# Recomputing two operand sums on VectorE instead of parking them in DRAM, and respacing the inner products of a Strassen-style token MLP

## The chip, the cores and the metric

The kernel runs on one core of a Trainium2 chip. The time is device microseconds (us) of that core, as the median of several executions. The profile's span, from the first to the last instruction, is about 2 us shorter than this time. A program on one core has no second, slower state to be told apart by its dies; every run used here was classed as fast, with a granted TensorE clock of 0.996 to 1.0. The executions at 0.996 or 0.997 are among the longest of their kernel (e11, which is after once more: 576.9 us at 0.997, 574.84 to 575.15 at 1.0). In the profile of that one the MLP starts 2.0 us later than in after, at 237.37 against 235.35 us, and its stages agree with those of after within 0.01 us. So medians and upper ends carry this difference at the start; the lengths of stages do not.

## The reference

The block is a linear attention layer, then a token-mixing MLP, each with a residual. Shapes: S = 2048 tokens, D = 1024, F = 3584, bfloat16. Only the second half matters here:

```
h  = x + attention(layernorm(x))
n  = layernorm(layernorm(h))              # S x D
u  = gelu(einsum("sd,sf->df", n, w1) + b1)   # first MLP matmul
y  = einsum("df,fs->ds", u, w2) + b2         # second MLP matmul
out = h + transpose(y)
```

## The kernel before

Both MLP matmuls are done by Strassen-Winograd products: seven products (1 to 7) of 128-row blocks instead of eight. The moving operand of the second matmul is g, the GELU output, kept as even rows `gE` and odd rows `gO`. Products 6, 7 and 4 need sums T2, T3 and T4 of g's blocks. `combine` makes them, row pair by row pair, as the first matmul ends each one:

```python
def combine(e, o, t2, t3, t4):
    lo, hi = slice(0, CW), slice(CW, 2 * CW)
    sub = ALU.subtract
    nc.vector.tensor_tensor(t3, o[:, hi], e[:, hi], sub)
    nc.vector.tensor_tensor(e[:, hi], e[:, hi], e[:, lo], sub)
    nc.vector.tensor_tensor(t2, o[:, hi], e[:, hi], sub)
    if t4 is not None:
        nc.vector.tensor_tensor(t4, o[:, lo], t2, sub)
# ... class Mixer1 (first matmul): after product 4 of row pair p
def done(self):
    p = self.p
    if p < NFP - 2:
        sg = stg.tile([P, 3, CW], FP16, tag="sg", name="sg")
        combine(gE[:, p, :], gO[:, p, :], sg[:, 0, :], sg[:, 1, :], sg[:, 2, :])
        nc.sync.dma_start(g_park[0][:, p, :, :], sg[:])      # parked in DRAM
```

The three sums are not kept in SBUF side by side: T2 is loaded once, and T3 and T4 take turns in one pair of tiles, reloaded from DRAM each time:

```python
def stream(m, t):                    # m = 7: T3, m = 4: T4
    def load():
        ts = stream_tiles()          # one buffer of each half
        nc.sync.dma_start(ts[0][:], g_park[0][:, 0:H2, t, :])
        # ... two more loads for the other half
        bind(m, ts)
    return load
```

Row pairs are worked in quads (two pairs). In a quad, products 1 and 5 of the two pairs together (in the second matmul only product 5) are themselves replaced by seven half-size inner products i1 to i7 (256 columns). These share two PSUM banks and hand partial sums on by ScalarE copies, so plain matmuls (512 columns) are placed between them:

```python
lo, hi = list(range(nk // 2)), list(range(nk // 2, nk))
def halves(fs):
    hs = [lambda f=f, ks=ks: f(ks) for f in fs for ks in (lo, hi)]
    return hs + [nop] * (4 - len(hs))
def interleave(n, fs):               # fs: products of the two pairs
    x = halves(fs)
    for f in (n.i1, x[0], n.i6, n.i2, x[1], n.i5, n.i7, x[2], n.i3, x[3], n.i4):
        f()
```

In the first matmul each x is 4 plain matmuls. The order of instructions on each engine is set by a scheduler that follows the program's order only loosely. The second matmul opens with two pairs done one after the other (`run_pair`), then runs quads.

## Time and profile before

Median 582.98 us (582.48 to 584.5, 4 runs). Three lines of the page: the span, the busy time of each engine, and the busy share of the DMA engines in 40 slices of the span, in tenths.

```profile
span 580.8 us, 8190 instructions
...
PE 568.5 (98%) x3061; PEld 287.2 (49%) x3061; DVE 363.0 (63%) x755; ACT 252.5 (43%) x547; POOL 1.8 (0%) x8
...
DMA  9934321149428652105144160549798897886415
```

Matmuls look 98% busy, but that hides gaps. One 128x512 matmul is recorded at 379 ns while matmuls in a run start 216 ns apart, so an idle stretch of up to 0.16 us disappears under the tail of the matmul before. The Trainium skill ("Perfetto Trace Analysis", "Identifying the Most-Contended Engine") says as much: matmul busy share is not a good measure of the distance to the limit. I therefore compare the time of a stage with its matmul count at the observed rates (about 216 ns for 512 columns and 109 ns for 256; the last column uses unrounded rates).

| stage of before | start, us | takes, us | at the observed rates, us |
|---|---|---|---|
| opening pairs of the first matmul | 235.54 | 23.97 | 22.44 |
| quad 1 (one pending pair) | 259.51 | 23.01 | 21.6 |
| quad 2 | 282.52 | 23.52 | 23.34 |
| quads 3, 4, 5 | 306.04 | 24.27, 24.40, 24.40 | 23.34 each |
| quad 6 and the last product 4 | 379.11 | 27.66 | 26.8 |
| first pairs of the second matmul, up to its first inner product | 406.77 | 51.97 | 48.35 |
| two steady quads of the second matmul | 458.74 | 41.61, 41.60 | 41.6 |

The windows view of before; columns are the stretch, its length, busy us of each engine with counts, clock, DMA share, GB/s. The rows are quads 3 to 5, the first pairs of the second matmul, and its two steady quads.

```profile
core 0: us, PE busy (x) PEld busy (x) DVE busy (x) ACT busy (x) POOL busy (x), PEclk, DMA share, GB/s
...
306.04:379.11 73.07, 71.70 (x410) 39.88 (x409) 43.87 (x97) 32.84 (x73) 0.00 (x0) 1.00 0.36 119
406.77:458.74 51.97, 49.25 (x226) 21.90 (x225) 30.96 (x41) 5.28 (x9) 0.00 (x0) 1.00 0.92 261
458.74:541.95 83.21, 83.21 (x435) 42.46 (x434) 39.72 (x52) 8.22 (x18) 0.00 (x0) 1.00 0.81 232
```

The largest MLP waits of the matmul engine (who waited, for what: total us, times, longest):

```profile
PE psC_4755 L285 <- DMA gs_4704<-g_park_2908: 0.8, 1, 0.8
...
PE psA_2922 L285 <- ACT psB_2923 L304: 0.7, 1, 0.7
PE psC_4610 L285 <- ACT psC_4610 L321: 0.7, 1, 0.7
...
PE psC_4755 L285 <- DMA gs_4798<-g_park_2908: 0.5, 1, 0.5
...
PE psI_3799 L218 <- ACT psA_3795 L419: 0.3, 1, 0.3
```

`gs` are the reloaded sums. The timeline of the start of quad 4, with the matmul engine's idle time in brackets:

```profile
330.31 0.60 PE L218 MATMUL psI_3799<-hE,wq 128*128 128x256 f16 x4
330.75 1.03 PE L285 MATMUL psC_3668<-hT_2232,wq 128*128 128x512 f16 x4
331.99 0.60 PE L218 MATMUL psI_3800<-hi_2916,is 128*128 128x256 f16 x4 [0.21 <-ACT psI_3800 L228]
...
332.86 1.03 PE L285 MATMUL psC_3668<-hT_2232,wq 128*128 128x512 f16 x4
334.17 0.60 PE L218 MATMUL psI_3799<-hE,is 128*128 128x256 f16 x4 [0.28 <-ACT psA_3795 L419]
```

i6 should have followed the four plain matmuls at 331.61 and started at 331.99. i5 should have started at 333.72 and started at 334.17. Both wait for ScalarE copies (L228, L419).

### The profile page before, as it was taken

Reading aid. Unit: us, or ns where it says so; the run is one execution under the profiler, and the core shown is the slowest. Engines: PE = TensorE matmul, PEld = TensorE weight load, DVE = VectorE, ACT = ScalarE, POOL = GpSimd, SP = SyncE. Lnnn points to the kernel's source line nnn. Section 1 sums busy time; section 2 is a strip of 40 time slices with the busy share of each in tenths; the row PEclk is TensorE's granted clock in tenths of the full one; section 3 lists DMA queues with packets and bytes.
Section 4 is the critical chain, followed back from the end, with each engine's and each line's share of the span. In section 5 each row is a group of like instructions: output and inputs, shape, how many; then the busy total and the mean of one; then the engine's idle time right before and its main releaser. Section 6 shows DMA issues by size and latency. Waiting matters only on the chain.

```text
span 580.8 us, 8190 instructions
## 1 busy us (share of the span) xinstructions
PE 568.5 (98%) x3061; PEld 287.2 (49%) x3061; DVE 363.0 (63%) x755; ACT 252.5 (43%) x547; POOL 1.8 (0%) x8
## 2 busy tenths in 40 slices
PE   8999999999999999999999999999998999999997
PEld 3444444455554444345555455554443554544544
DVE  6898878556678889774755738452575328236323
ACT  5657777756668767444535354354110110100100
POOL 1000000000000000000000000000000000000000
PEclk9999999999999999999999999999999999999999
DMA  9934321149428652105144160549798897886415
GB/s 305 351 69 90 93 55 37 20 150 311 82 57 166 173 170 85 43 29 172 32 168 143 57 200 28 172 126 314 196 300 278 271 305 235 228 229 217 146 31 169
DMA packets 119784, 91.52 MB, mean 158 GB/s; under 512 B 32818, under 2 KB 112192, under 8 KB 119744
## 3 DMA queue, kind: packets, MB, share of 16 engines
q1 hardware_dynamic: 119008, 90.32, 54.2%
q10 hardware_dynamic: 672, 0.66, 0.3%
q8 instruction: 24, 0.39, 0.3%
q14 instruction: 16, 0.13, 0.1%
q0 software_dynamic: 64, 0.01, 0.0%
HBM read 70.00 MB, written 13.63 MB: 144 GB/s over the span
## 4 chain that ended last, share of the span: by engine, by line
PE 73%; DMA 10%; DVE 9%; ACT 4%; issue 2%; SPq 0%; ACTq 0%; DVEq 0%
PE acc_t L963 9%; PE acc_t L1111 9%; DMA wq<-in_B_w_dram 6%; PE psB L694 4%; PE psC L694 4%; PE psA L694 4%; DVE sa L277 2%; PE psE L694 2%; PE nd_ps L1062 1%; DMA xr<-in_A_x_dram 1%; PE psC_4610 L285 1%; DMA gs_4633<-g_park_2908 1%; ACT gO L355 1%; PE psB_4544 L285 1%; PE psA_5495 L285 1%
## 5 line engine op out<-in xcount | busy, mean ns | idle before, releaser
L285 PEld LDWEIGHTS <-sa 128*128 128x128 f16 x716 | 70.0, 98 | 80.1 <-issue 3.8
L285 PEld LDWEIGHTS <-wq 128*128 128x128 bf16 x590 | 57.2, 98 | 63.0 <-issue 2.5
L963 PE MATMUL acc_t<-xnT,wq_sb 128*128 128x512 bf16 x256 | 58.0, 379 | 0.0
L1111 PE MATMUL acc_t<-wo_sb,pqT 128*128 128x512 bf16 x256 | 56.1, 379 | 0.0
L277 DVE TENSOR_TENSOR sa<-wq 128x1024 f16<-128x1024 bf16 (+1 forms) x44 | 36.1, 829 | 19.6 <-DMA wq<-in_B_w_dram 14.9
L1111 PEld LDWEIGHTS <-pqT 128*128 128x128 bf16 x256 | 24.9, 98 | 29.0
L963 PEld LDWEIGHTS <-wq_sb 128*128 128x128 bf16 x256 | 24.5, 98 | 27.4
L166 ACT ACTIVATE e_sb<-acc_t 128x512 bf16<-128x512 f32 x40 | 23.9, 597 | 26.6 <-PE acc_t L963 24.3
L218 PEld LDWEIGHTS <-is 128*128 128x128 f16 x276 | 26.9, 97 | 16.9 <-issue 6.3
L170 DVE TENSOR_SCALAR e_sb<-e_sb 128x512 bf16<-128x512 bf16 x64 | 18.5, 289 | 25.3 <-ACT e_sb L166 24.8
L694 PEld LDWEIGHTS <-xs 128*128 128x128 f16 x208 | 20.1, 98 | 23.3 <-DVE xs L680 1.3
L694 PE MATMUL psA<-wkv,xnT 128*128 128x512 bf16 x104 | 26.7, 379 | 0.0
L1122 DVE BATCH_NORM_STATS2 hst<-acc_t 128x6 f32<-128x512 f32 x32 | 22.1, 693 | 6.7 <-ACT h_bf L1121 6.5
L1109 ACT CAST acc_t<-xr 128x512 f32<-128x512 bf16 x32 | 19.0, 593 | 13.4 <-DVE hst L1122 13.3
L277 DVE TENSOR_TENSOR sa<-wq,sa 128x1024 f16<-128x1024 bf16 (+1 forms) x22 | 18.3, 830 | 10.4 <-PE psI_4907 L218 3.1
L694 PEld LDWEIGHTS <-xnT 128*128 128x128 bf16 x156 | 15.3, 98 | 18.5 <-issue 0.2
L167 ACT ACTIVATE r_sb<-acc_t 128x512 bf16<-128x512 f32 x40 | 23.7, 593 | 0.0
L618 PE MATMUL acc_t<-wkv,xnT 128*128 128x512 bf16 x96 | 21.6, 379 | 0.7 <-ACT xnT L871 0.7
L1083 DVE TENSOR_TENSOR o_sb<-nd_ps,rd 128x384 bf16<-128x384 f32 (+1 forms) x48 | 21.7, 504 | 0.6 <-ACT rd L1078 0.4
L587 DVE BATCH_NORM_STATS2 st<-x_sb 128x6 f32<-128x512 bf16 x32 | 20.5, 681 | 1.6 <-DMA x_sb<-in_A_x_dram 1.6
L1121 ACT CAST h_bf<-acc_t 128x512 bf16<-128x512 f32 x32 | 18.4, 574 | 1.0 <-PE acc_t L1111 0.9
L277 DVE TENSOR_TENSOR sa<-sa,wq 128x1024 f16<-128x1024 f16 (+1 forms) x22 | 18.2, 829 | 0.0
(711 smaller groups left out, 959.0 us busy)
## 6 DMA issues: line engine op xcount, KB each, us to landing
wq<-in_B_w_dram SPq DMA_DIRECT2D x14, 1024.0 KB, 7.9
wq<-in_B_w_dram SPq DMA_DIRECT2D x8, 1792.0 KB, 12.1
g_park_2908<-sg SPq DMA_DIRECT2D x12, 384.0 KB, 3.8
xr<-in_A_x_dram SPq DMA_DIRECT2D x16, 256.0 KB, 3.0
out_dram<-ot SPq DMA_DIRECT2D x31, 128.0 KB, 3.4
x_sb<-in_A_x_dram SPq DMA_DIRECT2D x15, 256.0 KB, 3.3
wkv<-in_A_wqkv_dram SPq DMA_DIRECT2D x2, 1024.0 KB, 9.0
wq_sb<-in_A_wqkv_dram SPq DMA_DIRECT2D x2, 1024.0 KB, 13.6
```

The source lines that it names most:

```text
L166: pin(nc.scalar.activation(e_sb[:], src, ACT.Exp))
L167: pin(nc.scalar.activation(r_sb[:], src, ACT.Relu))
L218: nc.tensor.matmul(ps, lhsT=self.lhs[m][:, k, :], rhs=self.mov[m][:, k, :], start=(start and k == 0), stop=(k == self.nk - 1), skip_group_ ...
L277: return nc.vector.tensor_tensor(t, a, b, op)
L285: nc.tensor.matmul(ps[:, cols], lhsT=lhs[:, k, :], rhs=mv(k)[:, cols], start=(start and k == 0), stop=(k == self.nk - 1), skip_group_check ...
L587: return nc.vector.bn_stats(st[:, c, :], x_sb[:, c * CW:(c + 1) * CW])
L618: mm = nc.tensor.matmul(pp[:, 0:CW], lhsT=xnT[:, kt, i * P:(i + 1) * P], rhs=wkv[:, kt, c * CW:(c + 1) * CW], start=(kt == 0), stop=(kt == ...
L694: pin(nc.tensor.matmul(ps[:], lhsT=lhs[:, k, :], rhs=rhs[:, k, :], start=(start and k == 0), stop=(k == hk2 - 1), skip_group_check=True,))
L963: nc.tensor.matmul(qp[:, 0:SW], lhsT=wq_sb[:, kt, j * P:(j + 1) * P], rhs=xnT[:, kt, u * SW:(u + 1) * SW], start=(kt == 0), stop=(kt == ND ...
L1083: nc.vector.tensor_tensor(o_sb[:, b * JPB * P:(b * JPB + nsl) * P].rearrange("p (s h e) -> p s h e", h=HB, e=DH), blk[:, :, 0:P].rearrange ...
L1111: nc.tensor.matmul(ap_[:, 0:CW], lhsT=pqT[:, j, i * P:(i + 1) * P], rhs=wo_sb[:, j, dc * CW:(dc + 1) * CW], start=(j == 0 and not SEED_RES ...
L1122: nc.vector.bn_stats(st[:, dc, :], ap_[:, 0:CW])
```

## The change

The intent is to stop parking T2, T3 and T4. Only the in-place subtraction stays in the first matmul. T2 is made once on VectorE at the switch. T3 and T4 are made anew for each quad, in place of each reload. The plain matmuls between the inner products are spread 5, 4, 3, 4. Two smaller reorderings come along: the first two pairs of the second matmul go jointly, and in opening pairs product 2 is split around product 6. Cut to its core:

```diff
         def done(self):
-            p = self.p
-            if p < NFP - 2:
-                sg = stg.tile([P, 3, CW], FP16, tag="sg", name="sg")
-                combine(gE[:, p, :], gO[:, p, :], sg[:, 0, :], sg[:, 1, :], sg[:, 2, :])
-                nc.sync.dma_start(g_park[0][:, p, :, :], sg[:])
+            e = gE[:, self.p, :]
+            nc.vector.tensor_tensor(e[:, CW:D], e[:, CW:D], e[:, 0:CW], ALU.subtract)
 ...
             def interleave(n, fs):
-                x = halves(fs)
-                for f in (n.i1, x[0], n.i6, n.i2, x[1], n.i5, n.i7, x[2], n.i3, x[3], n.i4):
-                    f()
+                steps = [(f, k) for f in fs for k in range(nk)]
+                t = len(steps)
+                cuts = [0, (5 * t + 8) // 16, (9 * t + 8) // 16, (12 * t + 8) // 16, t]
+                ...                      # fill(q) runs steps[cuts[q]:cuts[q + 1]]
+                for f in (n.i1, 0, n.i6, n.i2, 1, n.i5, n.i7, 2, n.i3, 3, n.i4):
+                    fill(f) if isinstance(f, int) else f()
 ...    # run_pair without a pending pair
-            for ks in (head, last):
-                st.p5(ks)
-                st.p2(ks)
+            st.p5(list(range(st.nk - 1)))
+            st.p2(list(range(h)))
+            st.p5([st.nk - 1])
 ...    # after product 6
+        st.p2(None if pend else list(range(h, st.nk)))
 ...    # second matmul
-    load_t3, load_t4 = stream(7, 1), stream(4, 2)
+    def derived(m, of):
+        def make():
+            ts = [g2pool.tile([P, H2, CW], FP16, tag=f"gs{h}", name=f"gs{h}") for h in range(2)]
+            for h, sl in enumerate(spans):
+                nc.vector.tensor_tensor(ts[h][:], *of(sl), ALU.subtract)
+            gmov[m] = lambda k: ts[k // H2][:, k % H2, :]
+        return make
+    make_t3 = derived(7, lambda sl: (gT2[:, sl, :], gE[:, sl, 0:CW]))
+    make_t4 = derived(4, lambda sl: (gO[:, sl, 0:CW], gT2[:, sl, :]))
 ...    # first two pairs: products 1, 5, 2, 6 of each, then 7 of both, then 3 of both
```

More of the change, by code (lines that the diff above doesn't have):

```diff
@@ L448, in run, with fill @@
             nk = self.sts[0].nk
-            lo, hi = list(range(nk // 2)), list(range(nk // 2, nk))
-            def halves(fs):
-                hs = [lambda f=f, ks=ks: f(ks) for f in fs for ks in (lo, hi)]
-                return hs + [nop] * (4 - len(hs))
             def interleave(n, fs):
-                x = halves(fs)
-                for f in (n.i1, x[0], n.i6, n.i2, x[1], n.i5, n.i7, x[2], n.i3, x[3], n.i4):
-                    f()
+                steps = [(f, k) for f in fs for k in range(nk)]
+                t = len(steps)
+                cuts = [0, (5 * t + 8) // 16, (9 * t + 8) // 16, (12 * t + 8) // 16, t]
+                def fill(q):
+                    part = steps[cuts[q]:cuts[q + 1]]
+                    for f in fs:
+                        ks = [k for g, k in part if g is f]
+                        if ks:
+                            f(ks)
+                for f in (n.i1, 0, n.i6, n.i2, 1, n.i5, n.i7, 2, n.i3, 3, n.i4):
+                    fill(f) if isinstance(f, int) else f()
             if self.mov1 is not None:
@@ L504, in run_pair @@
         if not pend:
-            head, last = list(range(st.nk - 1)), [st.nk - 1]
-            for ks in (head, last):
-                st.p5(ks)
-                st.p2(ks)
+            h = st.nk // 2
+            st.p5(list(range(st.nk - 1)))
+            st.p2(list(range(h)))
+            st.p5([st.nk - 1])
         else:
@@ L517, in run_pair @@
         nxt.pre(6)
-        if pend:
-            st.p2()
+        st.p2(None if pend else list(range(h, st.nk)))
         before_p7()
@@ L1187 @@
     assert NFP % 2 == 0 and NSP % 2 == 0 and NSP >= 4 and NFP >= 6
-    g_park = [dram.tile([P, n, 3, CW], FP16, name=f"g_park{t}") for t, n in enumerate((NFP - 2, 2))]
     inner1 = mctx.enter_context(tc.tile_pool(name="inner1", bufs=1, side="right"))
     pools["is"] = inner1
-    stg = mctx.enter_context(tc.tile_pool(name="stg", bufs=2, side="right"))
     hmov.update(moving(hE, hO, hT2, hT3, hT4))
@@ L1216 @@
         pend, nxt = cur.run(pend, lambda: quad1(u + 1) if u + 1 < NQ1 else None, on_p4=next_load1(u + 1))
-    last2 = pend
-    for st in last2:
+    for st in pend:
         st.p4()
@@ L1227 @@
     pools["is"] = inner2
-    NK = NFP - 2
     H2 = NFP // 2
     gT2 = g2pool.tile([P, NFP, CW], FP16, name="gT2")
-    def stream_tiles():
-        return [g2pool.tile([P, H2, CW], FP16, tag=f"gs{h}", name=f"gs{h}") for h in range(2)]
-    def bind(m, ts):
-        gmov[m] = lambda k: ts[k // H2][:, k % H2, :]
-    def stream(m, t):
-        def load():
-            ts = stream_tiles()
-            nc.sync.dma_start(ts[0][:], g_park[0][:, 0:H2, t, :])
-            nc.sync.dma_start(ts[1][:, 0:NK - H2, :], g_park[0][:, H2:NK, t, :])
-            nc.sync.dma_start(ts[1][:, NK - H2:H2, :], g_park[1][:, :, t, :])
-            bind(m, ts)
-        return load
-    load_t3, load_t4 = stream(7, 1), stream(4, 2)
-    nc.sync.dma_start(gT2[:, 0:NK, :], g_park[0][:, :, 0, :])
-    ts = stream_tiles()
-    nc.sync.dma_start(ts[0][:], g_park[0][:, 0:H2, 1, :])
-    nc.sync.dma_start(ts[1][:, 0:NK - H2, :], g_park[0][:, H2:NK, 1, :])
-    gmov.update(moving(gE, gO, gT2, None, None))
-    bind(7, ts)
-    cur = Mixer2(0)
-    for m in (5, 6, 7, 3):
-        cur.asum(m)
-    for t, st in enumerate(last2):
-        p = st.p
-        sg = outp.tile([P, CW], FP16, tag="sg", name="sg")
-        combine(gE[:, p, :], gO[:, p, :], gT2[:, p, :], ts[1][:, p - H2, :], sg[:])
-        nc.sync.dma_start(g_park[1][:, t, 1, :], ts[1][:, p - H2, :])
-        nc.sync.dma_start(g_park[1][:, t, 2, :], sg[:])
+    spans = (slice(0, H2), slice(H2, NFP))
+    cur = Mixer2(0)
+    cur.asum(5)
+    for sl in spans:
+        nc.vector.tensor_tensor(gT2[:, sl, :], gO[:, sl, CW:D], gE[:, sl, CW:D], ALU.subtract)
+    for m in (6, 7, 3):
+        cur.asum(m)
+    gmov.update(moving(gE, gO, gT2, None, None))
+    def derived(m, of):
[7 more added lines that the diff above has]
+    make_t4 = derived(4, lambda sl: (gO[:, sl, 0:CW], gT2[:, sl, :]))
     load_w2(1, wpool)
@@ L1272, in act @@
         def act():
-            load_t3()
+            make_t3()
             for p in (2 * u + 2, 2 * u + 3):
@@ L1277, in after_p4 @@
         return act
-    cur.prefetch()
-    nxt = Mixer2(1)
-    pend = run_pair(cur, [], nxt, on_p7=load_t4)
-    cur, nxt = nxt, quad2(1)
-    cur.prefetch()
-    pend = run_pair(cur, pend, nxt, after5=sums5, on_p4=load_t3, on_p7=load_t4)
+    pend = [cur, Mixer2(1)]
+    nxt = quad2(1)
+    for st in pend:
+        st.prefetch()
+        if st is pend[1]:
+            for m in (5, 6, 7, 3):
+                st.asum(m)
+            make_t3()
+        st.p1()
+        st.p5()
+        st.p2()
+        st.p6()
+    sums5()
+    nxt.pre(5)
+    for st in pend:
+        st.p7()
+    make_t4()
+    nxt.pre(6)
+    nxt.pre(7)
+    for st in pend:
+        st.p3()
+    nxt.pre(3)
     for u in range(1, NSP // 2):
@@ L1290 @@
             pend, lambda: None if last else quad2(u + 1),
-            on_p4=after_p4(u), on_p7=load_t4, cut=CW - P if last else None,
+            on_p4=after_p4(u), on_p7=make_t4, cut=CW - P if last else None,
         )
```

## The prediction

> **What bounds it.** The page gives the matmul engine 98% of the 580.8 us span at full clock; the wait view finds only about 10 us of idle, of which some 2.5 us at the start and 3 us in the tail are out of the change's reach. But a 128x512 matmul is recorded at 379 ns while matmuls of one run start 216 ns apart (14 in 3.02 us, timeline), and 128x256 ones 109 ns apart. That agrees with the Trainium skill, "TensorE: Matmul & The Clock Gate", "Wait — 56ns, not 53.3ns?" (215.7 ns at N = 512). So gaps up to 0.16 us are hidden in busy time, and I count gaps from starts instead:
>
> - First MLP matmul, quads: a quad is 80 plain and 56 half-width matmuls, 23.34 us at those rates. Quads 3 to 5 take 24.3 to 24.4 us (starts 306.0, 330.3, 354.7, 379.1), quad 2 23.5, quad 1 and quad 6 lose 1.4 and 0.9. Sum of gaps about 5.5 us. In the quad at 330 us: 0.38 before the second inner product (it waits for ScalarE's bank copy, queued behind two GELUs), 0.44 before inner product 5 (copy late behind a GELU that VectorE fed late), 0.06 before product 3, 0.15 in the second inner set.
> - First MLP, opening pair: about 1.5 us, mostly on a ScalarE copy.
> - Start of the second matmul: 406.77 to 458.74 us holds 224 plain matmuls, 48.35 us: 3.6 us of gaps, named by the waits as DMA loads of parked sums (0.8, 0.5, 0.5) and a ScalarE copy (0.7).
> - Steady second-matmul quads: starts 500.35 to 541.95, no gap.
>
> **What changes.** No matmul is added or removed. Removed: 12 parking stores of 384 KB, the 1.5 MB reload of gT2 and some eight reloads of 1.5 to 1.75 MB. VectorE loses about 42 subtractions of 128x512 (0.335 us each from start to start), 14 us, mostly from the first matmul. It gains gT2 plus two sums for each of four quads. 128x1792 f16 takes 1.0 us, so 128x3584 is estimated at 1.95: 3.9 us for each full sum, 35 us in all. VectorE's busy time should go from 363 to about 384 us.
>
> **Critical path.** (1) The fifth matmul hides 0.2 us in front of the second inner product in both inner sets; and with the parking subtractions gone, VectorE feeds the last GELU earlier, so the copy before inner product 5 comes sooner. I expect 0.5 to 0.8 us per quad, 3.4 us in all. The gap narrowed to three should just fit VectorE's 0.42 us sum. (2) The joint first pair with T3 made locally: 2.9 of 3.6 us. gT2 is ready near 412, needed at 416. (3) Opening pair: 0.2 us. (4) Steady quads: VectorE was busy 22.7 of 42 us; 7.8 more makes 73%. T3 has some 17 us until product 7, T4 some 12 until product 4, so nearly all is off the path; I allow 0.3 us for late sums.
>
> Sum: 6.2 us gained, 576.8 us. Range 574.3 to 579.8. Removing every gap listed would give about 572.5, so 2% is out of reach: faster 0.02, same 0.96, slower 0.02.
>
> **Signs.** Matmul count equal; first-matmul quads 23.5 to 23.9 us; the stretch from the second matmul's start to its first inner product about 49 us; no parked-sum DMA in the waits; VectorE about 384 us; DMA share in the second half down from 0.9 to about 0.6; steady quads still 41.6 us.
>
> **What would make it wrong.** The scheduler ordering the 3.9 us sums ahead of the small ones that free banks (steady quads over 42 us); late second-layer weights at the switch; product 3 now waiting with only three matmuls ahead.

## More of the kernel before

The weights of the next quad are loaded by SyncE's queue when the last product 4 has released their buffer (`next_load1`: two halves of 1 MB).

Last, the chain of waits of before, over the period that ends in quad 4. Columns are the start, the duration and what ran. It is followed back from the end of the program, so each line released the next.

```profile
313.79 0.43 DVE sg L159
...
314.24 0.32 SPq L370
...
314.61 8.01 DMA wq<-in_B_w_dram
...
322.71 0.42 DVE is L210
...
332.14 0.70 DVE t_3788 L362
...
334.17 0.60 PE psI_3799 L218 x4
...
337.48 0.68 ACT gO L355
...
338.18 0.44 DVE sg L159
...
338.63 0.32 SPq L370
...
339.00 8.11 DMA wq<-in_B_w_dram
```

Read it as a loop. The GELU of product 4 (`gO`) feeds the parking subtraction (`sg`), this releases the parking store (L370), behind the store goes the weight load (`wq`, 8.0 us), then VectorE makes the next quad's sums, and far behind these come its product sum (`t`), the last GELUs and a ScalarE copy, for which i5 waits; then product 4 again. One turn, from load to load, is 339.00 - 314.61 = 24.39 us: just the length of quad 4.

## The result and the profile after

Median 574.93 us (574.82 to 575.22, 4 runs), against 582.98 before. The ratio is 0.9858 (95% interval 0.984 to 0.9877). A ratio is the mean time of one kernel's fast runs over that of the other's of the same rounds, so it is not quite the ratio of the medians. 8.05 us were gained where 6.2 were predicted, inside the predicted range. The same page lines, of after:

```profile
span 573.1 us, 8081 instructions
...
PE 566.0 (99%) x3061; PEld 287.2 (50%) x3061; DVE 383.8 (67%) x731; ACT 254.7 (44%) x547; POOL 1.8 (0%) x8
...
DMA  9934432039536762104041240425971852842001
```

The span fell by 7.7 us and matmul busy time by only 2.5 us: two thirds of the closed gaps were visible as idle, one third had been hidden in "busy". The windows view of after, for the same stages:

```profile
core 0: us, PE busy (x) PEld busy (x) DVE busy (x) ACT busy (x) POOL busy (x), PEclk, DMA share, GB/s
...
305.15:375.86 70.71, 70.71 (x410) 39.91 (x409) 37.90 (x79) 34.13 (x73) 0.00 (x0) 1.00 0.28 90
402.88:451.23 48.35, 48.35 (x226) 21.91 (x225) 40.12 (x39) 5.28 (x9) 0.00 (x0) 1.00 0.61 158
451.23:534.45 83.22, 83.22 (x436) 42.46 (x435) 55.14 (x61) 8.22 (x18) 0.00 (x0) 1.00 0.50 135
```

All waits of the matmul engine that the profile lists for after:

```profile
PE acc_t L94 <- DVE warm L86: 1.2, 1, 1.2
PE tp L862 <- DVE xn L598: 0.8, 1, 0.8
PE psA_2917 L285 <- ACT psB_2918 L304: 0.7, 1, 0.7
PE acc_t L619 <- ACT xnT L872: 0.7, 2, 0.4
PE psB L695 <- DVE xs L681: 0.3, 1, 0.3
```

Only one of them (L285, the opening pair's ScalarE copy) lies in the MLP. The timeline of the start of a quad of after, quad 3:

```profile
305.15 0.60 PE L218 MATMUL psI_3541<-hE,wq 128*128 128x256 f16 x4
305.58 1.24 PE L285 MATMUL psC_3410<-hT_2232,wq 128*128 128x512 f16 x5
306.66 0.60 PE L218 MATMUL psI_3542<-hi_2911,is 128*128 128x256 f16 x4
...
307.54 0.81 PE L285 MATMUL psC_3410<-hT_2232,wq 128*128 128x512 f16 x3
308.19 0.38 PE L285 MATMUL psC_3436<-hT_2232,wq 128*128 128x512 f16 x1
308.40 0.60 PE L218 MATMUL psI_3541<-hE,is 128*128 128x256 f16 x4
```

i6 follows its five plain matmuls with no gap (305.58 + 5 x 0.216 = 306.66), and i5 follows at once too. The chain of waits of after, over the start of the next quad, is matmuls behind matmuls; the loop through the weight load is gone:

```profile
328.88 0.44 PE psI_3764 L218 x4
329.32 1.08 PE psC_3633 L285 x5
```

Where the 7.7 us of span went:

| stage | before | after | gained |
|---|---|---|---|
| up to the first matmul's start | 235.54 | 235.35 | 0.19 |
| opening pairs | 23.97 | 23.81 | 0.16 |
| quad 1 | 23.01 | 22.42 | 0.59 |
| quad 2 | 23.52 | 23.57 | -0.05 |
| quads 3 to 6 with the last product 4 | 100.73 | 97.73 | 3.00 |
| first pairs of the second matmul | 51.97 | 48.35 | 3.62 |
| two steady quads | 83.21 | 83.22 | -0.01 |
| last quad and tail | 38.83 | 38.65 | 0.18 |

### The profile page after: what moved, and what is told of

Same layout as the page of the kernel before. It is cut to its first block, busy times and chain, and to the rows that moved or that the text cites. A ratio compares the mean times of both kernels' runs of the same rounds, so it can differ in the third digit from the quotient of the medians.

```text
span 573.1 us, 8081 instructions
## 1 busy us (share of the span) xinstructions
PE 566.0 (99%) x3061; PEld 287.2 (50%) x3061; DVE 383.8 (67%) x731; ACT 254.7 (44%) x547; POOL 1.8 (0%) x8
## 4 chain that ended last, share of the span: by engine, by line
PE 93%; DVE 3%; DMA 2%; ACT 2%; issue 1%; SPq 0%; ACTq 0%
PE acc_t L964 9%; PE acc_t L1112 9%; PE psB L695 4%; PE psC L695 4%; PE psA L695 4%; PE psE L695 2%; PE nd_ps L1063 1%; DMA xr<-in_A_x_dram 1%; PE psB_4758 L285 1%; PE psC_5500 L285 1%; PE psC_5181 L285 1%; PE psB_5064 L285 1%; PE psC_4858 L285 1%; PE psA_4757 L285 1%; PE psC_4527 L285 1%; PE psB_4550 L285 1%
## 5 line engine op out<-in xcount | busy, mean ns | idle before, releaser
L285 PEld LDWEIGHTS <-sa 128*128 128x128 f16 x716 | 70.0, 98 | 77.3 <-issue 0.7
L285 PEld LDWEIGHTS <-wq 128*128 128x128 bf16 x590 | 57.1, 98 | 61.7 <-issue 1.0
```

Of the source, the lines that this page charges most:

```text
L285: nc.tensor.matmul(ps[:, cols], lhsT=lhs[:, k, :], rhs=mv(k)[:, cols], start=(start and k == 0), stop=(k == self.nk - 1), skip_group_check ...
```

## The experiments

Twelve runs, in three groups of four; each group shared one chip and the runs of before on it (medians of before: 582.42, 582.18 and 582.5 us). Each run was timed in five rounds, and each result was correct. Two theories stood for the first matmul. **P**, the prediction's spacing argument: the fifth plain matmul hides 0.2 us in each inner set. **V**, its other half: the parking subtractions kept VectorE from feeding the last GELU in time. For the second matmul, **D**: it is the local sums that close the gaps, and **J**: it is the joint order with half the reloads.

Stages of the runs that bear on these theories, from their profiles (us); e7, e8, e11 and e12 are told in the text. "Sums at" is when VectorE begins the next quad's sums, measured from the start of quad 3; the profile has it waiting for the weights just before. "Quad 4" is the length of the quad that follows.

| run | median | quad 1 | sums at | quad 4 | first pairs, 2nd matmul | steady quad |
|---|---|---|---|---|---|---|
| before | 582.98 | 23.01 | 16.67 | 24.40 | 51.97 | 41.61 |
| e1 spacing only | 581.71 | 22.44 | 16.63 | 24.22 | 51.46 | 41.61 |
| e9 parked on another queue | 584.13 | 24.39 | 16.71 | 24.34 | 51.27 | 41.61 |
| e3 joint, streamed | 580.20 | 23.01 | 16.84 | 24.40 | 49.43 | 41.61 |
| e6 stores, no subtractions | 577.09 | 22.42 | 16.15 | 23.96 | 48.35 | 41.61 |
| e5 subtractions, no store | 575.07 | 22.43 | 14.71 | 23.58 | 48.35 | 41.61 |
| after | 574.93 | 22.42 | 14.59 | 23.57 | 48.35 | 41.61 |
| e10 parked after the loads | 579.35 | 23.20 | 14.57 | 23.53 | 52.80 | 41.61 |
| e2 old spacing | 575.81 | 23.50 | 14.45 | 23.52 | 48.34 | 41.61 |
| e4 apart, local | 575.02 | 22.42 | 14.62 | 23.56 | 48.35 | 41.60 |

### e1: the new spacing alone, in the kernel before

```diff
-            lo, hi = list(range(nk // 2)), list(range(nk // 2, nk))
-            def halves(fs): ...
-            def interleave(n, fs): ...     # of before
+            def interleave(n, fs): ...     # of after
```

> The kernel before with only the new spacing of the inner products; parking, reloads and the opening order of before are kept. Theory P (as predicted: the fifth matmul hides 0.2 us in front of the second inner product, in both inner sets): steady quads of the first matmul 23.9 to 24.0 us instead of 24.3 to 24.4, about 2 us gained, near 581. Rival V (what emptied the gaps is the parking subtractions leaving VectorE; a matmul moved in front of the second inner product is taken from in front of product 3 and only moves the gap): quads 24.2 to 24.4, less than 0.7 us gained, 582.3 to 583.2. Second matmul as before, 52 us to its first inner product.

Measured: 581.71 us (581.3 to 582.33), ratio 0.9984 (0.9964 to 1.0004). Quads 3 to 5 took 24.26, 24.22 and 24.55 us. P falls. What the spacing did gain is in quad 1, 0.57 us: that quad has only one pending pair, so the old code had two halves for four places and left the places in front of products 3 and 4 empty. The new cuts give each place something.

### e2: the old spacing, in the kernel after

```diff
-            def interleave(n, fs): ...     # of after
+            lo, hi = ...; def halves(fs): ...; def interleave(n, fs): ...   # of before
```

> The kernel after with the spacing of before (halves); all else as after. Theory P: about 2 us slower than after, quads 23.9 to 24.0 us, near 577. Rival V: quads 23.5 us, as in the one quad of before that had no GELU queue (282.5 to 306.0), so within 0.5 us of after, 574.5 to 575.4. Second matmul stays at 48.35 us to its first inner product.

Measured: 575.81 us (575.59 to 577.14), ratio 0.9886 (0.9864 to 0.9908). Quads 2 to 5 took 23.51 to 23.52 us, 0.05 us less than with the new spacing; quad 1 took 1.08 us more. So the spacing is worth about 0.9 us in after, all of it in quad 1. P is rejected a second time. The quads fit what was written for V (23.5 us); the total does not quite: it lies above V's 574.5 to 575.4, by the loss in quad 1, which neither theory foresaw. That V's cause was still wrong is shown by e5.

### e3: joint first pairs, sums still reloaded

```diff
-    pend = run_pair(cur, [], nxt, on_p7=load_t4)
-    ...
-    pend = run_pair(cur, pend, nxt, after5=sums5, on_p4=load_t3, on_p7=load_t4)
+    pend = [cur, Mixer2(1)]
+    ...                                   # the joint opening of after
+        st.p7()
+    load_t4()
```

> The kernel before, but the first two steps of the second matmul run jointly as in after, with sums still parked and reloaded: each sum is loaded once for the two steps, not once for each. Theory J (the order and the halved number of reloads close the 3.6 us of gaps, not the place where the sums come from): 48.4 to 49.5 us instead of 51.97 from the start of the second matmul to its first inner product, 2.5 to 3.6 us gained, 579.5 to 580.6. Theory D (a reload after product 7 cannot land before product 4 while weights are loading, and only VectorE can make the sum in time): 50.5 us or more, under 1.5 us gained.

Measured: 580.2 us (579.72 to 580.54), ratio 0.9957 (0.9938 to 0.9977). The stretch took 49.43 us: 2.54 of the 3.6 us came back, as J had it (48.4 to 49.5). Its wait list has no DMA wait any more; the 0.7 us wait for ScalarE's copy is still there.

### e4: separate first pairs, sums made locally

```diff
-    pend = [cur, Mixer2(1)]
-    ...                                   # the joint opening
+    make_t3()
+    pend = run_pair(cur, [], nxt, on_p7=make_t4)
+    cur, nxt = nxt, quad2(1)
+    cur.prefetch()
+    pend = run_pair(cur, pend, nxt, after5=sums5, on_p4=make_t3, on_p7=make_t4)
```

> The kernel after, but the first two steps of the second matmul run one after the other as in before, each with T3 and T4 made on VectorE. Theory D (local sums close the gaps whatever the order): 48.4 to 49.5 us to the first inner product, 575 to 576. Theory J (the order closes them): still over 50.5 us, 577 or more. In both, the wait for ScalarE's copy of the bank in front of the first step's product 7 (0.7 us in before) comes back, since product 7 follows product 6 directly.

Measured: 575.02 us (574.86 to 575.03), ratio 0.9867 (0.9844 to 0.9891), 48.35 us for the stretch, the same as after. The joint order adds nothing to what e4 has. The two causes overlap: order alone brings 2.54 us; local sums with separate pairs and the new split of product 2 bring all of it. The expected 0.7 us wait did not come back. Its timeline shows why: the new split of product 2 leaves seven plain matmuls between products 6 and 7. In e3, which kept a whole product 2 in front of product 6 in its actual order, product 7 came right behind product 6. In after, the first product 7 comes only behind the second pair's product 6 (427.05 us), so there too no copy is waited for. Local sums with neither the split nor the joint order were not run: of the 3.62 us, the DMA waits (1.9 us) are the sums' to close, but this 0.7 us is closed by the order of products.

### e5: the parking subtractions without the stores, in the kernel after

```diff
         def done(self):
-            e = gE[:, self.p, :]
-            nc.vector.tensor_tensor(e[:, CW:D], e[:, CW:D], e[:, 0:CW], ALU.subtract)
+            if p < NFP - 2:
+                sg = stg.tile([P, 3, CW], FP16, tag="sg", name="sg")
+                combine(gE[:, p, :], gO[:, p, :], sg[:, 0, :], sg[:, 1, :], sg[:, 2, :])
+            # else: the one subtraction, as in after
```

> The kernel after, with the three parking subtractions for each of the first twelve row pairs put back on VectorE (into a scratch tile that nothing reads) and no store. Theory V (VectorE's time in front of the last GELU makes ScalarE's bank copies late): the steady quads of the first matmul go back to 24.2 to 24.5 us from the third on, as in the run with only the spacing, about 3 us lost, 577.5 to 578.5. Rival S (the stores and their tile's release were what delayed things): quads stay at 23.57, 575.

Measured: 575.07 us (574.84 to 575.22), ratio 0.9874 (0.986 to 0.9889). Quads 23.58 to 23.59 us. The page shows that VectorE did do the work, 12.5 us more than in after:

```profile
PE 566.5 (99%) x3061; PEld 287.1 (50%) x3061; DVE 396.3 (69%) x767; ACT 254.5 (44%) x547; POOL 1.8 (0%) x8
```

V falls: 12 us of subtractions, at the very place where they stood, cost nothing.

### e6: the stores without the subtractions, in the kernel after

```diff
             nc.vector.tensor_tensor(e[:, CW:D], e[:, CW:D], e[:, 0:CW], ALU.subtract)
+            if self.p < NFP - 2:
+                nc.sync.dma_start(g_park[:, self.p, 0:D], gO[:, self.p, :])
+                nc.sync.dma_start(g_park[:, self.p, D:D + CW], e[:, 0:CW])
```

> The kernel after, with as many bytes stored to DRAM for each of the first twelve row pairs as before (384 KB, straight from gO and gE), no subtractions added and nothing read back. Theory V: quads stay at 23.57, 574.6 to 575.4. Rival S: quads of 24 us or more, 577 or more.

Measured: 577.09 us (576.86 to 577.41), ratio 0.991 (0.9895 to 0.9925). Quads 3 to 5 took 23.95 to 23.97 us, quad 6 with its products 4 took 28.02 against 27.02. So it is the stores that the loss needs, and that calls for a new theory. Two limits of this run: from quad 3 to the last product 4 it brings back 2.17 us of the 3.00, not all. And what went out between the two halves of the load was the 256 KB from `gO` alone (the stores from `gE` followed more than 8 us later). The second half of the load went out 7.85 us after the start of quad 3, against 8.57 in before, where the store also has to wait for a 0.43 us subtraction (`sg` in the chain). So the subtractions, which cost nothing alone, probably add to the delay where a store waits for them; no run separates this from the smaller store. On SyncE's queue in before, a store stands in front of each half of the next quad's weight load (start, duration, what was issued):

```profile
311.20 0.32 SPq L370 DMA_DIRECT2D g_park_2908<-sg  x1
313.06 0.38 SPq L140 DMA_DIRECT2D wq<-in_B_w_dram  x1
314.24 0.32 SPq L370 DMA_DIRECT2D g_park_2908<-sg  x1
314.61 0.43 SPq L140 DMA_DIRECT2D wq<-in_B_w_dram  x1
```

**Q**: the second store waits for the quad's last GELU, the second half of the load (314.61) waits behind it, and what the load feeds comes late, round and round, as the chain of before shows.

### e9 and e10: two ways to keep the stores away from the loads, in the kernel before

```diff
# e9
-                nc.sync.dma_start(g_park[0][:, p, :, :], sg[:])
+                nc.gpsimd.dma_start(g_park[0][:, p, :, :], sg[:])
# e10
-                nc.sync.dma_start(g_park[0][:, p, :, :], sg[:])
+                park.append(lambda: nc.sync.dma_start(g_park[0][:, p, :, :], sg[:]))
...     # end of load() in next_load1, after load_w1(u, 0) and load_w1(u, 1)
+            while park:
+                park.pop(0)()
```

> The kernel before with one word changed: the parking stores of the first matmul are issued from GpSimd's queue, not from SyncE's, where each stands in front of a half of the next quad's weight load. All subtractions, stores and reloads stay. Theory Q (the weight loads wait in SyncE's queue behind stores that wait for the quad's last GELU, so the next quad's sums, product sums, GELUs and bank copies all come late, round and round): quads 3 to 6 of the first matmul fall from 24.3 to 24.4 to 23.5 us, about 3 us gained, 579 to 580. Rival B (the stores' bytes slow the loads, whatever queue they are on): quads stay above 24 us, under 1 us gained.

> The kernel before with the parking stores still on SyncE's queue, but issued after the two halves of the next quad's weight load instead of between and in front of them. Theory Q: as the run with GpSimd's queue, quads of 23.5 us, 579 to 580. Rival B: no gain of over 1 us. If only this one gains and not the GpSimd one, the bytes matter and not the queue.

e10 measured: 579.35 us (578.93 to 580.15), ratio 0.994 (0.9923 to 0.9957). Quads 2 to 5 took 23.52 to 23.53 us with the old spacing, all subtractions, all stores and all reloads in place. SyncE's queue in e10, for the same quad (a line with x2 merges two issues, and its time runs to the end of the second):

```profile
310.41 0.34 SPq L371 DMA_DIRECT2D g_park<-sg  x1
312.26 1.01 SPq L140 DMA_DIRECT2D wq<-in_B_w_dram  x2
313.44 0.88 SPq L371 DMA_DIRECT2D g_park<-sg  x1
```

The scheduler left the first store in front. All that changed in the steady quads is that the second store now follows both halves of the load. The sums begin at 14.57 us instead of 16.67. Rival B (the stores' bytes slow the loads, whatever the queue) is rejected: every byte is still stored, and the second half of the load lands 7.77 us after its issue, as in after. Quads 1 to 6 with the last product 4 were 3.0 us shorter (144.26 against 147.26), and 0.83 us were given back at the switch (52.80 us against 51.97), where the waits for reloaded sums grew from 1.9 to 2.4 us.

e9 measured: 584.13 us (582.42 to 585.47), ratio 1.0017 (0.9995 to 1.0039). No gain, a miss for Q as I had put it, and what B had foretold. Its chain of waits shows the load landing 9.0 us after issue instead of 8.0, with the sums starting just as late as before:

```profile
316.21 8.99 DMA wq<-in_B_w_dram
...
325.22 0.42 DVE is L210
```

Another queue is no other road. The Trainium skill says it ("Trainium Kernel Development and Optimization", "Key Constraints": DMAs of the SP, ACT and POOL queues run on the same 16 DMA engines and interleave), and this run agrees, with a median landing of the first-matmul weight loads of 8.5 us against 7.9 in before and 7.7 in e10. The landings of single transfers show it best. In e10 the second store was issued 0.74 us after the second half of the load, on the same queue, and landed 0.9 us after it. In e9 it was issued 1.03 us after, on the other queue, and landed 1.0 us before it. So it is not the bytes as such, as the expectation of e10 would have it, but whether they move ahead of the load or beside it. One more thing changed in e9: the profile counts these stores as `software_dynamic` (q0), those from SyncE's queue as `hardware_dynamic` (q1). ScalarE's queue was not tried. What counts is when the second half of the weights has landed, and a store can delay that in two ways. Measured from the start of quad 3:

| run | second half issued at | lands after | sums at |
|---|---|---|---|
| after | 6.79 | 7.77 | 14.59 |
| before | 8.57 | 8.01 | 16.67 |
| e6 | 7.85 | 8.21 | 16.15 |
| e9 | 7.70 | 8.99 | 16.71 |

In before nearly all of the delay is the later issue (1.78 of 2.08 us, some 1.1 of it behind the second store). e9 took half of that away, 0.87 us: both halves now go out together (316.21 - 308.51 = 7.70 for the second), as soon as product 4 is done with the buffer, but product 4 is itself late in the loop. It lost the same again by a longer landing, beside the store. Quad 1 of e9 lost 1.4 us more: VectorE waited 2.0 us for the weights before the next quad's first sum (273.39 us), and a sum that the matmul engine needed came only behind it (273.73 us); the matmul engine waited 1.2 us for that.

### e7 and e12: spacing 5, 4, 4, 3

```diff
-                cuts = [0, (5 * t + 8) // 16, (9 * t + 8) // 16, (12 * t + 8) // 16, t]
+                cuts = [0, (5 * t + 8) // 16, (9 * t + 8) // 16, (13 * t + 8) // 16, t]
```

> The kernel after, with the matmul that was taken from in front of product 3 taken from in front of product 4 instead (5, 4, 4, 3). In after each quad still has about 0.1 us in front of product 3 in both inner sets (its three matmuls end before VectorE's sum of 0.42 us), and with the old halves 0.15 us in front of the second inner product of the second set. If product 4 waits only for sums already done, quads drop from 23.57 to 23.35 us, 1.1 us gained, 573.9. If product 4 waits for the sum after product 3, since both halves lie in one bank, the gap only moves again: 23.5 to 23.6, 575.

> The spacing 5, 4, 4, 3 once more, beside after on the same chip, since its first profile had a start-up wait of over 1 us: quads 23.48, opening as in after, 0.5 us (0.1%) faster than after, which the interval may or may not separate from 0.

> The kernel after unchanged, as a yardstick on the same chip for the next run: 574.5 to 575.3, first-matmul quads 23.57.

e7: 574.81 us (574.57 to 576.56), ratio 0.9869 (0.9852 to 0.9885). e12: 574.36 us (574.12 to 576.69), ratio 0.9865 (0.9843 to 0.9887). e11, after itself on that chip: 574.91 us (574.84 to 576.9), ratio 0.9869 (0.9849 to 0.989). Quads took 23.48 us in both runs against 23.57: most of the hoped-for 0.2 us did not come, and three small gaps of about 0.04 us each remain. The medians of e12 and e11 differ by 0.55 us, and the stages of the MLP by 0.5 us. The runs overlap only through the executions at 0.997: at 1.0, e12 took 574.12 to 574.36 us (3 runs) and e11 574.84 to 575.15 (4 runs). So it is likely faster than after, by 0.1%.

### e8: the local sums made twice, in the kernel after

```diff
-                nc.vector.tensor_tensor(ts[h][:], *of(sl), ALU.subtract)
+                for _ in range(2):
+                    nc.vector.tensor_tensor(ts[h][:], *of(sl), ALU.subtract)
```

> The kernel after, with each T3 and T4 made twice on VectorE with the same result, about 31 us more of VectorE work in the second matmul. Theory O (the local sums lie off the critical path with room to spare): steady quads 41.6 us, first pair 48.4 to 49, VectorE near 415 us, 575 to 576. Theory T (they only just fit): steady quads over 42 us, 577 or more.

Measured: 577.51 us (577.47 to 577.64), ratio 0.9917 (0.9902 to 0.9932). Steady quads of 42.28 and 42.18 us, 1.1 us more in the last quad and tail, the first pairs unharmed at 48.35. O is a miss and T is right. The wait that appears is the matmul engine waiting for VectorE's sum of product 5's inner products, 1.3 us in all:

```profile
PE psI L218 <- DVE e L428: 1.3, 3, 0.5
```

The local sums, 7.8 us for a quad of 41.6, cost nothing; twice as much costs 0.6 us a quad. The room is real and less than double.

## Why the prediction was right or wrong

**Total and range: right.** 576.8 predicted in 574.3 to 579.8, 574.93 measured. Of the 1.85 us by which the gain exceeds the forecast, 0.7 are the first pairs (3.62 where 2.9 stood), 0.3 the allowance for late sums that were not late, 0.1 the quads, and 0.4 lie before the MLP and in the tail, where nothing of the change acts; the rest is the difference between spans and medians.

**Step (1), the first matmul's quads: right in size, wrong in cause, so by luck.** The step read: "The fifth matmul hides 0.2 us in front of the second inner product in both inner sets; and with the parking subtractions gone, VectorE feeds the last GELU earlier". 3.4 us were forecast and 3.54 came. But e1 and e2 show that the fifth matmul brings nothing in quads 2 to 6 (it costs 0.05 us in each) and 0.6 to 1.1 us in quad 1, which the prediction had not linked to the spacing at all. e5 shows that the subtractions alone cost nothing. What cost 3 us was the second parking store in front of the second half of the weight load: e10 moves it and gets all of that back, e6 puts stores back and loses 2.2 us of it. The path that the step named (VectorE late, the last GELU late, the ScalarE copy late, inner product 5 waiting) is in the chain of before; what made VectorE late was the weights, for which it waited 3.4 us a quad (2.1 in after), and not the subtractions. The table of runs orders itself by one number: with the next sums started by 14.7 us after the quad's start, the following quad takes 23.52 to 23.58 us; from 16.15 us on, it takes 23.96 to 24.40.

**Step (2), the first pairs: right, undersized.** Local sums with the split of product 2 close all 3.62 us without the joint order (e4), which the step named first. The joint order alone closes 2.54 (e3).

**Step (3), the opening pair: right.** 0.16 us where 0.2 stood. e1, with the old opening order, kept 23.96 us; e2 and e5, with the new one, took 23.81 and 23.82, so it is that reordering.

**Step (4), steady quads: right.** 41.61 us, with VectorE at 27.6 of 41.6 us in a steady quad, 66% where 73% stood: the prediction's 22.7 us for before came from a window not cut at the quads (488 to 530); between the starts of quads it is 19.9. e8 shows that it would not have held for double the work.

**Signs.** VectorE 383.8 us (384 forecast), no parked-sum DMA in the waits, DMA share 0.61 and 0.50 in the two second-matmul windows, and 2% not reached: all as written. The narrowed gap in front of product 3 "should just fit"; it misses by about 0.1 us (309.27 + 3 x 0.216 = 309.92, product 3 at 310.03).

**What stays open.** Why the load takes 9.0 us beside a store on another queue was argued from the shared DMA engines and not tested further. What share of the delay in before comes from the subtraction for which the second store waits was not measured. e4 does not separate the first pairs fully, since the scheduler moved products across them. In e10 the larger waits for reloaded sums were seen and not explained.

## What to carry to other kernels

A store behind a prefetch cost nothing in the steady quads here (e10), but one that goes out in front of or beside it made it land later (before, e6, e9), and a chain that already fits only just then closes into a loop longer than the busiest engine's work. Put the loads first (e10: one store moved behind a load, 3 us), and do not count on another queue: GpSimd's did not help (e9). When a wait names an engine that is hardly busy, follow the chain further back than the wait list does: here the list said ScalarE and the chain said DMA. And a prediction that lands in its range has not shown its reasons: both reasons given for the largest forecast here were wrong, and only the experiments told.

## What the Trainium skill lacked or had wrong

- "TensorE: Matmul & The Clock Gate" (in the section "Wait — 56ns, not 53.3ns?"): agrees. It gives 215.7 ns from start to start for 512 columns; the trace has 14 in 3.02 us, 216 ns.
- "Perfetto Trace Analysis" ("Identifying the Most-Contended Engine"): its warning about matmul busy share agrees. The measures that it recommends instead, over a whole window, do not place the gaps. Here the span fell by 7.7 us and busy time by 2.5 us; starts against the matmul count, stage by stage, showed where.
- "VectorE: DVE Perf Modes": it sets its cycle count `58 + FD/Accel` (in "The TRN2 errata — SBUF-src ops pay a fixed extra latency per instruction") against the duration of one operation, which the count under-predicts, and does not say that it fits the time from start to start. Here a 128x512 fp16 subtraction is recorded at 0.42 us and the next one starts after 0.335 us, and a 128x3584 one at 2.02 us with the next after 1.94. The estimates from that row, at its 2x and 0.96 GHz, are 0.327 and 1.927 us.
- "Trainium Kernel Development and Optimization" ("Key Constraints"): its statement that another issuing queue brings no other DMA engines agrees with e9, where the load took longer beside the store. It has no number for what the sharing costs: a 1 MB load landed 9.0 us after issue beside a 384 KB store on another queue, against 8.0 behind it on the same queue and 7.8 ahead of it (e10).
